# A gated recurrent attention and feed-forward kernel: fixed order on every engine, q turned by TensorE, stack halves by GpSimd, convolution sums in PSUM

## Chip, core and metric

The kernel runs on one core of a Trainium2 chip. The core has a matrix engine (TensorE; its weight loads have a row of their own), VectorE, ScalarE and GpSimd, and DMA engines that are fed from the queue of SyncE (SP) and, for a few transfers, from ScalarE's. In the rows they are PE and PEld, DVE, ACT, POOL and SPq. TensorE writes to PSUM, eight banks of 2 KB per partition; the others work on SBUF, and VectorE and ScalarE on PSUM as well. The metric is the device time of one execution in microseconds.

## What is computed

Two layers, in f32. The first is a recurrence with matrix state per head (4 batches, 8 heads, 768 steps, 40 elements per head), the second a gated feed-forward layer over the 320 joined elements.

```python
for t in range(S):                                  # 768
    m_new = maximum(f_gate[t] + m, i_gate[t])
    f_stab = exp(f_gate[t] + m - m_new); i_stab = exp(i_gate[t] - m_new); m = m_new
    C = f_stab * C + i_stab * outer(v[t], k[t])     # 40 x 40 for each head
    n = f_stab * n + i_stab * k[t]
    y[t] = sigmoid(o_gate[t]) * (C @ q[t]) / maximum(abs(n . q[t]), 1)
gate = sigmoid(causal_conv(x, conv_w))              # x is y as 4 x 768 x 320; 5 taps along t, per channel
out  = (gate * (x @ w_val)) @ w_out
```

## The kernel before

The 768 steps are cut into six chunks `j` of 128, and each chunk into two halves `p` of 64. A chunk has four units `u`, one for each batch `b`; a unit has two groups `g`, one for each half. So there are 24 units and 48 groups, and a group treats the 8 heads of a batch for 64 steps.

**Preparation of a chunk.** `load_qk`, `load_v` and `load_o` read q, k, v and the output gate. `prep_max` (ScalarE) and `prep_scale` (VectorE) find a power-of-two scale for each row. Each f32 value is then held as a pair of f16 values, side by side in a stack tile `stk` of 3 x 40 columns for each head: `prep_hi` (GpSimd, L327) writes the high part, `prep_lo` (VectorE) writes the residual (L332) and a second copy of the high part (L341). `prep_tr` (L352) turns the stack from rows to columns by a DMA transpose on SP's queue: q goes to `tq`, k to `tk`. There are 24 stacks of q and 24 of k, two `stk` buffers, three `tk` and two `tq`. `load_k` moves a copy of k with its halves swapped into `kp`, by DMA except for the first two.

**A group.** `args` (TensorE, `psd`) and `expo` (ScalarE, `dm`) make the decay weights, `scores` (8 matmuls, `pss`) the products of q and k, `probs` (VectorE, `pt`) joins both, and `keyw` (GpSimd, `kw`) weights the keys. `heads` runs 8 matmuls into `ph`, the output, and between them 8 into `pc`, the new state, which `state_out` (ScalarE) writes beside the values in `vc`; the next group of that batch reads it from there. After two groups `norm` (VectorE), `norm_o` (GpSimd) and `gate_o` (VectorE) finish the unit, `x_tr` turns it on TensorE, and `x_copy` (ScalarE) and `x_rest` (GpSimd) put it and the last four steps of the chunk before it into `xc` and `x3`.

**Feed of a chunk.** The convolution has 5 taps for each of three channel blocks. The first tap writes the sum tile `sg` (`conv0`, GpSimd, L501; for the third block VectorE, L513), the other four add to it in SBUF (`conv`, VectorE, L514). Then follow `sigmoid` (ScalarE), `val` (TensorE, `pf`), `z_mul` (VectorE), and for each batch `outp` (TensorE, `po`), `outp_st` (ScalarE) and `out_dma`. For the last chunk the feed is made in two halves of two batches.

**Order and buffers.** A table LAGS gives each step a time relative to its group or chunk. The calls are sorted by that time and handed to a scheduler, which sets the order on each engine except SP's; `heads` keeps its own order on TensorE. PSUM is split into pools: five banks in turn for `psd`, `pss`, `px`, `pf` and `po`, two for `ph`, one for `pc`.

Of the kernel before, what the change touches and what calls it, by code (L numbers as in the profile page):

```python
# [16 lines left out]

LAGS = {  # L20
    "cons1": -5.183, "cons1d": 0, "cons2": 0.457, "cons2d": 2.675, "wgt": 3.44, "wgtd": 0.804, "close": 2.831,
    "og": -7.359, "kp": -5.611, "kpd": 1.009, "vc": -3.927, "vcd": 0.989, "nat": -14.361, "natd": 0.826,
    "sig_o": -3.584, "max": -9.51, "hi": -8.451, "lo": -6.85, "lod": 0.308, "tr": -5.254, "den": -0.323,
    "dend": 0.177, "rs": 1.457, "gate": 3.86, "x_tr": 4.721, "x_copy": 6.057, "x_rest": 7.056, "args": -3.401,
    "expo": -3.399, "scores": -2.076, "probs": -1.445, "keyw": -2.703, "state": -0.531, "state_out": 0.189,
    "heads": -0.632, "conv0": 4.698, "conv0d": 0.9, "conv": 5.393, "convd": 0.299, "sig": 8.436, "val": 8.878,
    "vald": 0.463, "z": 9.375, "zh": 9.181, "zl": 9.511, "outp": 13.042, "outpd": 0.257, "ob": 15.39, "od": 14.45,
    "sig0": -0.329, "maxd": 0.014, "early": 0.441, "conv3": 8.55, "scaled": 0, "e_conv0": 5.797, "e_conv0d": 0.226,
    "e_conv": 4.49, "e_convd": 0, "e_conv3": 3.873, "e_sig": 7.715, "e_val": 6.616, "e_vald": 0.359, "e_z": 8.556,
    "e_zh": 8.123, "e_zl": 8.811, "e_outp": 11.131, "e_outpd": 0.989, "e_ob": 9.909, "e_od": 11.211, "half": 2.582,  # L30
    "si1": 1.548, "og1": 4.264, "sig1": 4.352, "vc1": -3.33, "kpe": 0, "natq": -13.409, "natqd": 0, "qmax": -10.547,
    "qmaxd": 0.075, "qhi": -9.634, "qlo": -8.762, "qtr": -8.036, "qd": 1.073, "qmul": -9.356, "qout": -3.776,
    "kpi": 6.531, "qe1": 0.864, "nat2": 0.089, "og2": -0.141, "sig2": -0.871, "qe2": 0.725, "og3": -0.415,
    "tr3": 0.74, "kp0": -1.411, "si1q": 1, "on_act_hi": 0, "on_act_dup": 0, "on_dve_state": 0, "on_dve_out": 0,
    "on_dve_x": 0, "on_dve_xl": 0, "on_dve_rs": 0, "on_dve_kw": 0, "on_dve_zl": 0, "z@2": 13.103, "zh@2": 13.406,
# [882 lines left out]
```

## Time and profile before

| | |
|---|---|
| Median of three runs | 290.42 us (290.09 to 290.68) |
| Profiled execution, its own time | 291.05 us |
| Its span, first to last instruction | 289.30 us |
| Mean granted TensorE clock | 0.850 |
| Busy: TensorE / VectorE / ScalarE / GpSimd | 214.8 / 212.2 / 137.6 / 122.3 us |
| Share of 16 DMA engines, SP's queue | 78.4% |

Busy time is the time in which an engine works on at least one instruction. A share of the span says little by itself here, since the stages of the kernel have different limits; the rows further down therefore split the span. The granted clock is in parts of full speed, 2.4 GHz; the other level is 1.2 GHz. Times within the span are counted from its start.

### The profile page before, as it was taken

What the parts mean: (1) busy time and instruction counts of PE and PEld (TensorE: products, weight loads), DVE (VectorE), ACT (ScalarE), POOL (GpSimd) and SP (SyncE); (2) the same over time, 40 slices, a digit from 0 to 9 for tenths busy, and PEclk for the clock granted to TensorE, in tenths of its full rate; (3) what the DMA queues carried; (4) which work ended last, traced back from release to release, by engine and by line L of the source; (5) the groups of instructions that cost most, each with busy time, mean ns of one, the idle gap of its engine ahead of it and who ended that gap; (6) DMA issues with size and microseconds to landing.
All of it is one profiled execution on the core that took longest, in us unless ns stands there. A gap on an engine that the chain in (4) does not pass through costs nothing.

```text
...
## 1 busy us (share of the span) xinstructions
PE 214.8 (74%) x2301; PEld 147.8 (51%) x2301; DVE 212.2 (73%) x537; ACT 137.6 (48%) x302; POOL 122.3 (42%) x211
## 2 busy tenths in 40 slices
...
GB/s 139 151 143 202 100 181 166 193 185 134 173 176 213 212 164 145 106 179 205 168 58 113 212 212 199 109 37 136 238 150 168 104 3 2 47 44 3 91 15 76
DMA packets 145895, 38.70 MB, mean 134 GB/s; under 512 B 135176, under 2 KB 143752, under 8 KB 145864
## 3 DMA queue, kind: packets, MB, share of 16 engines
q1 hardware_dynamic: 143044, 37.76, 78.4%
...
## 4 chain that ended last, share of the span: by engine, by line
PE 38%; DVE 14%; DMA 6%; issue 6%; ACT 5%; POOL 2%; SPq 1%; DVEq 0%; ACTq 0%; POOLq 0%
PE po L567 9%; PE ph L442 6%; PE pf L546 5%; DVE sg L514 4%; PE po L568 4%; PE pf L542 3%; PE pss L389 3%; PE pf L548 2%; DMA sg<-in_o_gate_dram 2%; DVE stk L332 2%; DVE pt L396 2%; DMA tk<-stk 2%; ACT sg L528 2%; PE pf L555 2%; PE px L476 2%
## 5 line engine op out<-in xcount | busy, mean ns | idle before, releaser
L442 PE MATMUL ph<-vc,pt 128*64 128x41 f32 (+1 forms) x768 | 68.5, 257 | 18.4 <-ACT vc L424 12.3
L442 PEld LDWEIGHTS ph<-vc,pt 128*64 128x64 f32 (+1 forms) x768 | 60.8, 165 | 32.6 <-ACT vc L424 15.5
L444 PE MATMUL pc<-vc,kw 128*40 128x41 f32 (+1 forms) x704 | 51.4, 235 | 5.3 <-POOL kw L408 3.5
L389 PE MATMUL pss<-tq,tk 120*128 120x64 f16 x384 | 34.4, 266 | 23.5 <-DMA tq<-stk 6.7
L327 POOL TENSOR_SCALAR stk<-nat,scl 128x320 f16<-128x320 f32 x48 | 32.6, 685 | 43.6 <-DMA tk<-stk 23.7
L444 PEld LDWEIGHTS pc<-vc,kw 128*40 128x40 f32 (+1 forms) x704 | 45.5, 135 | 10.6 <-POOL kw L408 5.5
L408 POOL TENSOR_TENSOR kw<-kp,dm 128x320 f32<-128x320 f32 (+1 forms) x44 | 35.6, 811 | 30.5 <-PE ph L442 16.6
L389 PEld LDWEIGHTS <-tk 120*128 120x128 f16 x384 | 27.6, 132 | 31.7 <-issue 15.4
L332 DVE SCALAR_TENSOR_TENSOR stk<-nat,scl,stk 128x320 f16<-128x320 f32 x48 | 33.5, 697 | 12.6 <-POOL stk L327 12.5
L514 DVE SCALAR_TENSOR_TENSOR sg<-xc,cwt,sg 128x512 f32<-128x512 f32 (+1 forms) x56 | 39.9, 730 | 3.2 <-POOL sg L501 3.1
L396 DVE SCALAR_TENSOR_TENSOR pt<-pss,cmp,dm 128x512 f32<-128x512 f32 x48 | 35.4, 738 | 9.4 <-PE ph L442 6.8
L362 PE MATMUL psd<-ra,la 120*128 120x512 bf16 x48 | 22.9, 477 | 21.5 <-DMA la<-gda 18.5
L373 ACT ACTIVATE dm<-psd 128x512 f32<-128x512 f32 x48 | 28.5, 595 | 20.5 <-PE psd L362 8.8
L293 ACT ACTIVATE junk<-nat 128x320 bf16<-128x320 f32 x48 | 22.5, 468 | 30.4 <-DMA nat<-in_q_dram 17.0
L424 ACT COPY vc<-pc 40x328 f32<-40x328 f32 x44 | 18.6, 423 | 32.9 <-PE ph L442 18.3
L462 POOL TENSOR_TENSOR rs<-sg,den 128x320 f32<-128x320 f32 x24 | 19.1, 795 | 33.6 <-DVE den L457 23.7
L567 PE MATMUL po<-wo,zt 128*128 128x320 f32 x96 | 31.3, 456 | 0.0
L573 ACT COPY ob<-po 128x320 f32<-128x320 f32 x24 | 10.0, 424 | 38.5 <-PE po L568 24.6
L560 DVE TENSOR_TENSOR zt<-pf,sg 128x512 f32<-128x512 f32 (+2 forms) x21 | 11.3, 544 | 14.8 <-PE pf L548 10.5
L546 PE MATMUL pf<-xc,wv 128*128 128x512 f32 x40 | 20.2, 629 | 2.3 <-ACT x L486 2.3
L567 PEld LDWEIGHTS po<-wo,zt 128*128 128x128 f32 x96 | 17.3, 196 | 8.8 <-issue 3.8
L501 POOL TENSOR_SCALAR sg<-xc,cwt 128x512 f32<-128x512 f32 (+1 forms) x14 | 10.7, 768 | 17.6 <-DVE zt L560 14.8
...
## 6 DMA issues: line engine op xcount, KB each, us to landing
nat<-in_q_dram SPq DMA_DIRECT2D x24, 160.0 KB, 4.1
...
out_dram<-ob SPq DMA_DIRECT2D x24, 160.0 KB, 1.8
kp<-nat SPq DMA_DIRECT2D x22, 160.0 KB, 3.0
...
nat<-in_k_dram SPq DMA_DIRECT2D x4, 160.0 KB, 3.4
rawv<-in_moe_w_val_dram SPq DMA_DIRECT2D x4, 160.0 KB, 3.3
```

Of the source, the lines that this page charges most:

```text
L327: return nc.gpsimd.tensor_scalar(o, v, f, 1.0, op0=ALU.mult, op1=ALU.mult)
L332: nc.vector.scalar_tensor_tensor(t[:, :, lo : lo + D], part(j, x, i), scl[j % 2][:, x, i : i + 1], t[:, :, 0:D], op0=ALU.mult, op1=ALU.sub ...
L362: nc.tensor.matmul(psd, la[:, p, j, b], ra[:, :, j], start=True, stop=True,)
L373: nc.scalar.activation(dm, psd_[g], AF.Exp)
L389: nc.tensor.matmul(o, tk[h], tq[:, h], start=True, stop=True)
L396: nc.vector.scalar_tensor_tensor(pt, pss_[g], cmp_[j % 2][:, p, b : b + 1], dmt[g], op0=ALU.mult, op1=ALU.mult)
L408: (nc.vector if turn("on_dve_kw", b) else nc.gpsimd).tensor_mul(kw[0:n], kp[0:n, p, b * H : (b + 1) * H], dmt[g][0:n, :, L - 1 : L].to_bro ...
L442: nc.tensor.matmul(pht[u][p * L : (p + 1) * L, h], ptt[g][0:n, h], mv, start=True, stop=True)
L444: nc.tensor.matmul(pc[n0 : n0 + D, h], kwt[g][0:n, h], mv, start=True, stop=True)
L514: nc.vector.scalar_tensor_tensor(o, x, w, o, op0=ALU.mult, op1=ALU.add)
L546: nc.tensor.matmul(pf, wv[:, c, ms], x[:, c, :, 4:], start=(c == 0), stop=False)
L567: nc.tensor.matmul(pf, zz[0][:, c, b], wo[:, c], start=(c == 0), stop=False)
```

## The change

All pools, the scheduler and LAGS go. Each step is entered in a list under a kind and a running number, and a table PLAN gives every entry a place; the list is sorted by place, and every engine executes its own instructions in that order. A second table BANKS names one of the eight PSUM banks for every sum, so any bank can serve any step.

The 24 stacks of q and the four of k's first chunk are turned by TensorE, eight transposes into one f16 bank (`turn_pe`), and copied out by ScalarE (`turn_out`); the other 20 stacks of k still go by DMA. `prep_hi` writes both copies of the high part at once, so `prep_lo` keeps one instruction. All 24 moves into `kp` are GpSimd copies. The convolution's first tap goes from GpSimd (third block: VectorE) to ScalarE and writes a PSUM bank; taps 2 to 4 add there, and the last writes `sg`. The four last steps of a chunk are carried over for all batches at once (`halo`, 10 copies for 40). The third output weight block gets its own zero-padded tile `wo3`. There are more buffers: `tk` 4 for 3, `stk` 3 for 2, `dm` 4 for 3, `pt`, `kw` and `ob` 3 for 2.

```diff
+NTK, NSTK, NDM, NPT, NKW, NOB, OJ = 4, 3, 4, 3, 3, 3, 3
+PLAN = {
+    "ld_g": "6 0",
+    "sct": "166 358 598 699 917 989",
...
+BANKS = {
+    "turn": "1023543544261302344310373663",
...
+def TURN(j, x, i):
+    return 1 if x == 0 or j == 0 else 0
+def KP(j, p, i):
+    return 2
...
-    ctx.enter_context(tc.manual_schedule(engines={mybir.EngineType.SP}))
+    ctx.enter_context(tc.manual_schedule())
...
-        put = nc.scalar.copy if j == i == 0 else nc.vector.tensor_copy if j < T["kpe"] else nc.sync.dma_start
+        put = (nc.sync.dma_start, nc.scalar.copy, nc.gpsimd.tensor_copy, nc.vector.tensor_copy)[KP(j, p, i)]
...
-    def prep_hi(j, i, x):
-        o, v, f = stk[i % 2][:, x, :, 0:D], part(j, x, i), scl[j % 2][:, x, i : i + 1]
-        return nc.gpsimd.tensor_scalar(o, v, f, 1.0, op0=ALU.mult, op1=ALU.mult)
+    def prep_hi(j, x, i):
+        t, f = stack(j, x, i), scl[j % 2][:, x, i : i + 1]
+        o = t[:, :, 0:K3].rearrange("p h (c d) -> p h c d", d=D)[:, :, 0 : 2 + x : 1 + x]
+        v = part(j, x, i)[:, :, None, :].to_broadcast([P, H, 2, D])
+            nc.gpsimd.tensor_scalar(o, v, f, 1.0, op0=ALU.mult, op1=ALU.mult)
...
-        put = nc.scalar.copy if j > 0 and turn("on_act_dup", 2 * i + x) else nc.vector.tensor_copy
-        return put(t[:, :, dup : dup + D], t[:, :, 0:D])
...
+    def turn_pe(n, j, x, i):
+        t = bank("turn", n, 512).bitcast(F16).rearrange("p (h n) -> p h n", h=H)
+        pw[j, x, i] = t
+        for h in range(H):
+            nc.tensor.transpose(t[0:K3, h], stack(j, x, i)[:, h, 0:K3], ident16)
+
+    def turn_out(j, x, i):
+        put = nc.scalar.copy if TURN(j, x, i) == 1 else nc.vector.tensor_copy
+        put(turned(j, x, i)[0:K3], pw[j, x, i][0:K3])
...
+    def conv(n, j, c, t, b0, b1):
...
+        if t == 0:
+            nc.scalar.activation(o, x, AF.Copy, scale=w)
+        else:
+            nc.vector.scalar_tensor_tensor(
+                of(gt, c, b0, b1) if t == 4 else o, x, w, o, op0=ALU.mult, op1=ALU.add
+            )
...
+    order = range(len(work)) if not slot else sorted(range(len(work)), key=lambda n: slot[work[n][0]][work[n][1]])
+    for n in order:
+        kind, i, fn, a = work[n]
+        fn(*a)
```

Three places of the order follow, each as it stands before and after. In their rows a line number, the operation, the tile written, the tiles read and the shape are named; `pb` is a PSUM bank.

SP's queue in the opening, before: after the loads of the first q and k come two transposes, then the gathers of the gate terms `ra` and `la`.

```order
L193 DMA nat_81<-in_k_dram 128x8x40
L352 DMA_TRANSPOSE tq_231<-stk_112 128x8x128
L352 DMA_TRANSPOSE tk_98<-stk_112 128x8x128
L206 DMA vc_84<-in_v_dram 64x32x40
L275 DMA ra<-gdg_122 24x8x64
L277 DMA la<-gda_124 24x4x64 x2
L206 DMA vc_84<-in_v_dram 64x32x40
L352 DMA_TRANSPOSE tq_231<-stk_113 128x8x128
```

The same place after:

```order
L367 DMA sg<-in_o_gate_dram 128x32x40
L351 DMA nat_67<-in_q_dram 128x8x40
L351 DMA nat_67<-in_k_dram 128x8x40
L355 DMA nat_68<-in_q_dram 32x8x160 x2
L343 DMA la<-gda_138 24x4x64
L339 DMA ra<-gdg_136 24x8x64
L343 DMA la<-gda_138 24x4x64
L355 DMA nat_68<-in_q_dram 32x8x160 x2
```

The transposes are gone from this queue, the output gate and part of the next q stand ahead of the gathers, and the first transpose of the program comes much later, for k of the second chunk.

TensorE at the first scores of chunk 2, before: the second group's scores (`pss_1351`) follow the first group's (`pss_1285`) with only an `args` between, and q has come by DMA.

```order
L389 LDWEIGHTS tk_100
L389 MATMUL pss_1285<-tq_951,tk_100 128x4x16
L362 LDWEIGHTS la
L362 MATMUL psd_1337<-ra,la 128x512
L389 LDWEIGHTS tk_100
L389 MATMUL pss_1351<-tq_951,tk_100 128x4x16
```

TensorE ahead of the scores of chunk 2, after: the value product of chunk 0 (L616, L607, L609) stands here, and then the first transposes of chunk 2's q (L447).

```order
L616 MATMUL pb_127<-xc_78,wall 64x256 x4
L616 MATMUL pb_127<-x_80,wall 64x256 x2
L607 MATMUL pb_125<-xc_78,wall 128x512 x2
L609 MATMUL pb_125<-x_80,wall 128x256 x2
L607 MATMUL pb_130<-xc_78,wall 128x512 x2
L609 MATMUL pb_130<-x_80,wall 128x256 x2
L447 LDWEIGHTS stk_92
L447 MATMUL pb_124<-ident_66,stk_92 120x128
```

Before, the first value product comes behind the first scores and heads of chunk 2. After, 16 of the 28 turned stacks come behind the 16th group of heads. At the other end, 32 value matmuls and 18 of the first two products of `outp` come behind the last heads before, 18 and 10 after.

VectorE at the first stack of the opening, before: the residual (L332) is followed by the second copy of the high part (L341), as every residual is.

```order
L305 TENSOR_SCALAR cmp_101<-amx_110 64x1 x2
L710 COPY la<-tl 120x2x512
L711 COPY ra<-tr 120x8x64
L332 SCALAR_TENSOR_TENSOR stk_112<-nat_81,scl_108,stk_112 128x8x40
L341 COPY stk_112<-stk_112 128x8x40
```

VectorE in the preparation of chunk 2, after: a residual (L424) stands alone, behind the last taps of chunk 0 (L575; a tap adds into a bank, a block's last one writes `sg`) and steps that convert the weights (L649 to L656).

```order
L575 SCALAR_TENSOR_TENSOR sg<-x_80,cwt,pb_126 128x256
L575 SCALAR_TENSOR_TENSOR pb_129<-xc_78,cwt,pb_129 128x512
L654 SCALAR_TENSOR_TENSOR wall<-cv_146,cv_145 128x320
L575 SCALAR_TENSOR_TENSOR sg<-xc_78,cwt,pb_129 128x512
L649 TENSOR_SCALAR cv_145<-raw_143 128x320
L650 SCALAR_TENSOR_TENSOR cv_145<-raw_143,cv_145 128x320
L656 SCALAR_TENSOR_TENSOR wall<-cv_147,wall 128x320
L651 TENSOR_SCALAR cv_146<-cv_145 128x320
L424 SCALAR_TENSOR_TENSOR stk_91<-nat_67,scl_97,stk_91 128x8x40
```

The second copy has left VectorE for GpSimd's wider `prep_hi`. Of the taps 2 to 5, 4 stand ahead of the 16th group of heads now.

## Rows read from the trace of the kernel before

**Rows 1.** Three stretches: length; PE, PEld, DVE, ACT, POOL busy; clock; DMA share; GB/s.

```profile
0.00:18.50 18.50, 0.00 (x0) 0.00 (x0) 15.97 (x54) 7.20 (x17) 12.34 (x33) 1.00 0.79 136
18.50:115.00 96.50, 54.58 (x716) 43.32 (x717) 76.72 (x201) 49.09 (x112) 45.44 (x73) 0.66 1.09 174
115.00:289.30 174.30, 160.18 (x1588) 104.48 (x1586) 119.55 (x284) 81.33 (x173) 64.55 (x106) 0.94 0.65 111
```

**Rows 2.** The same view of shorter stretches, with the same columns.

```profile
18.50:46.00 27.50, 13.68 (x185) 10.61 (x185) 24.10 (x60) 15.88 (x33) 10.38 (x19) 0.74 1.03 167
...
80.00:115.00 35.00, 20.82 (x262) 16.62 (x261) 31.57 (x77) 17.01 (x41) 20.82 (x30) 0.60 1.15 185
115.00:150.00 35.00, 28.69 (x349) 20.50 (x349) 29.35 (x76) 21.39 (x49) 18.36 (x28) 0.77 0.98 148
150.00:183.00 33.00, 30.66 (x368) 20.74 (x365) 22.30 (x53) 19.33 (x44) 14.42 (x24) 0.95 0.98 167
183.00:207.00 24.00, 23.80 (x272) 15.50 (x271) 19.21 (x52) 10.81 (x20) 13.06 (x24) 1.00 0.77 118
```

**Rows 3.** Waits of the whole span: us in total, times, longest.

```profile
POOL stk L327 <- DMA tk<-stk: 23.7, 10, 4.9
...
POOL stk L327 <- DMA tq<-stk: 8.7, 5, 2.8
```

**Rows 4.** DMA issues: count, KB each, median us to landing.

```profile
kp<-nat SPq DMA_DIRECT2D x22, 160.0 KB, 3.0
...
tq<-stk SPq DMA_TRANSPOSE x24, 3.8
tk<-stk SPq DMA_TRANSPOSE x24, 4.8
```

**Rows 5.** Timeline of the opening: start, us, engine, line, what.

```profile
13.66 1.95 SPq L275 DMA_DIRECT2D ra<-gdg  x1
...
15.80 0.77 SPq L277 DMA_DIRECT2D la<-gda  x2
...
18.54 0.59 PE L362 MATMUL psd<-ra,la 120*128 120x512 bf16 x1 [18.54 <-DMA la<-gda]
```

**Rows 6.** Chain that ended last (start, us); L476's ns min/median/max.

```profile
231.57 0.55 PE pss L389 x8
...
255.24 0.48 PE px L476 x3
...
L476 PE MATMUL px<-ident,x x72: 272/273/475, 52.8 to 258.4; 128*128 128x128 f32 x48, 128*64 128x128 f32 x24
```

**Rows 7.** Groups by form: busy us, mean ns | idle before, releaser.

```profile
L514 DVE SCALAR_TENSOR_TENSOR sg<-xc,cwt,sg 128x512 f32<-128x512 f32 x40 | 32.8, 823 | 2.5 <-POOL sg L501 2.5
...
L327 POOL TENSOR_SCALAR stk<-nat,scl 128x320 f16<-128x320 f32 x48 | 32.6, 685 | 43.6 <-DMA tk<-stk 23.7 <-DMA tq<-stk 8.7 <-DVE scl L300 5.3
...
L332 DVE SCALAR_TENSOR_TENSOR stk<-nat,scl,stk 128x320 f16<-128x320 f32 x48 | 33.5, 697 | 12.6 <-POOL stk L327 12.5
...
L341 DVE COPY stk<-stk 128x320 f16<-128x320 f16 x48 | 14.8, 307 | 0.0
...
L202 ACT COPY kp<-nat 64x640 f32<-64x640 f32 x2 | 1.4, 722 | 0.0
```

**Rows 8.** VectorE in the middle stretch: L341's instructions alone, then L514's.

```profile
18.50:115.00 96.50, 5.32 (x23) 0.66 1.09 174
...
18.50:115.00 96.50, 8.43 (x12) 0.66 1.09 174
```

**Rows 9.** Lines L396, L332, L514: ns min/median/max, first and last start.

```profile
L396 DVE SCALAR_TENSOR_TENSOR pt<-pss,cmp,dm x48: 693/738/753, 22.1 to 245.1; 128x512 f32<-128x512 f32 x48
...
L332 DVE SCALAR_TENSOR_TENSOR stk<-nat,scl,stk x48: 493/550/1133, 9.1 to 221.3; 128x320 f16<-128x320 f32 x48
...
L514 DVE SCALAR_TENSOR_TENSOR sg<-xc,cwt,sg x56: 466/737/1633, 88.9 to 269.7; 128x512 f32<-128x512 f32 x40, 128x256 f32<-128x256 f32 x16
```

**Rows 10.** Chain that ended last: start, us, the last heads.

```profile
252.18 1.06 PE ph L442 x16
```

More of the change, by code (lines that the diff above doesn't have):

```diff
@@ new lines, in tile_mlstm_gated_ffn, with op, bank @@
+    x_ = ring(2, [P, H, D], F32, "x")
+    obt = cst.tile([P, NOB * DM], F32, name="ob")
+    ob_ = [obt[:, i * DM : (i + 1) * DM] for i in range(NOB)]
+    pb = [ps.tile([P, 512], F32, name=f"pb{i}") for i in range(8)]
+    work, seen = [], {}
+    def op(kind, fn, *a):
+        i = seen[kind] = seen.get(kind, -1) + 1
+        work.append((kind, i, fn, a))
+    turns = {}
+    def bank(kind, i, n, m=None):
+        if kind in BANKS:
+            b = int(BANKS[kind][i])
+        else:
+            b = turns["b"] = (turns.get("b", -1) + 1) % 8
+        t = pb[b][:, 0 : n * (m or 1)]
+        return t.rearrange("p (a b) -> p a b", b=m) if m else t
@@ L569, in outp @@
-        pot[(j, b)] = pf
+        r = slice(0, P) if j < NJ - 1 else half(b)
+        nc.tensor.matmul(pf, zz[1][r, b % B2], wo3[r, b // B2], start=False, stop=True)
     def outp_st(j, b):
-        ob = wk.tile([P, DM], F32, name=f"ob{j}_{b}", tag="ob", bufs=2)
-        (nc.vector.tensor_copy if turn("on_dve_out", b) else nc.scalar.copy)(ob, pot[(j, b)])
-        pot[(j, b)] = ob
+        nc.scalar.copy(ob_[(j * B + b) % NOB], pot[j, b])
     def out_dma(j, b):
-        nc.sync.dma_start(out[b, j * P : (j + 1) * P, :], pot[(j, b)])
@@ L882, in tile_mlstm_gated_ffn @@
-    for j in range(NJ - 1):
-        feed(j, (j + 1) * SJ, 0, B)
-    for i in range(2):
-        feed(NJ - 1, NG + T["half"] * i, 2 * i, 2 * i + 2, "e_")
-    for _, _, fn, a in sorted(work, key=lambda w: w[:2]):
+            if x == 0:
+                nc.vector.tensor_reduce(sel_b, i4, axis=AX.X, op=ALU.add)
+            else:
+                nc.vector.tensor_reduce(sel_g, i4.rearrange("p b g -> p g b"), axis=AX.X, op=ALU.add)
+    MS, VS = nc.gpsimd.memset, nc.vector.memset
+    op("ld_g", nc.sync.dma_start, fg, f_gate.rearrange("b h s -> (b h) s"))
@@ new lines, in tile_mlstm_gated_ffn @@
+    op("c_p", make_identity, nc, ident)
+    op("c_v", nc.vector.tensor_copy, ident16, ident)
+    op("c_p", MS, io_, 0.0)
+    for r0 in (0, 2 * D):
+        op("c_p", fill, io_[:, 0:D], [[-1, D]], -r0)
+    for i in range(NTK):
+        for x in range(2):
+            op("idk", idk, i, x)
+    for x in range(2):
+        op("sums", sums, x)
+    op("c_p", MS, kp[0:L, 0], 0.0)
+    for p in range(2):
+        op("kp_c", kp_const, p)
+    for i in range(2):
+        op("c_p", MS, vc[i][0:L, 0], 0.0)
+        for p in range(2):
+            op("c_p", MS, vc[i][TOK[p] : TOK[p] + L, p, :, D:DT], 1.0)
@@ new lines, in feed_part @@
+    def feed_part(j, b0, b1):
+        for c in range(3):
+            n = seen.get("conv0", -1) + 1
+            for t in range(5):
+                op("conv" if t else "conv0", conv, n, j, c, t, b0, b1)
+        op("sig", sigmoid, j, b0, b1)
+        for m in range(3):
+            op("val", val, seen.get("val", -1) + 1, j, m, b0, b1)
+            op("z", z_mul, j, m, b0, b1)
+        for b in range(b0, b1):
+            op("outp", outp, j, b)
+            op("ob", outp_st, j, b)
+            op("od", out_dma, j, b)
```

974 lines of the change are left out of this document (459 added, 515 removed), and 74 rows, old and new, of tables (LAGS, PLAN).

## The prediction

> **What bounds the kernel now.** I read the trace by stretches first, because no engine is the limit throughout. [rows 1] cuts the span where the first TensorE work starts (18.5 us) and where 16 of the 48 head groups are done (115 us; counted from the `ph` matmuls). The reader is to compare each engine's busy time with the length of its stretch. In the middle stretch (96.5 us) TensorE is busy 54.6, at a granted clock of 0.66, ScalarE 49.1 and GpSimd 45.4; VectorE is busy 76.7, and the DMA engines stand at 1.09 of their capacity. In the last stretch (174.3 us) TensorE is busy 160.2: it is the bound there, with the DMA share down to 0.65. [rows 2] refines that: VectorE reaches 0.88 (24.10 of 27.50) and 0.90 (31.57 of 35.00) of two slices of the middle, and at 115 to 150 us it is still level with TensorE (29.35 and 28.69 of 35); from 150 us TensorE is at 0.93 and then 0.99, with the clock back at 1.00.
>
> Next I asked what keeps VectorE from being full in the middle. The waits [rows 3] name DMA transposes: GpSimd stands 23.7 and 8.7 us because the stack buffers it must refill are still being read by a transpose. A transpose lands 3.8 or 4.8 us after its issue [rows 4], and two stack buffers do not cover that. So the middle is bound by VectorE through a chain that DMA latency keeps opening, and the end by TensorE.
>
> **The change part by part.** The sum is made against the profiled execution: span 289.30 us, its own time 291.05, so 1.75 lies around the span. Its time is 0.63 above the median of the three runs, 290.42.
>
> *Opening, 18.5 us.* The gathers of the gate terms are issued at 13.66 and 15.80 us, behind two transposes on SP's queue, and TensorE's first matmul waits for the last of them until 18.54 [rows 5]. The new queue has no transpose ahead of them. The latest gather can go out about 2.1 us earlier (15.80 to 13.66), but VectorE and GpSimd get more constants and wider stacks first. Bounds 16.4 and 18.5; I take 17.5.
>
> *Transposes of q and of the first k.* 28 of 48 leave the DMA queue. On TensorE each is 8 matmul-type instructions of 128 columns, f16. No row shows that form. From below: the eight score matmuls, with the same kind of weight load but 64 columns, take 0.55 us [rows 6]. From above: three f32 transposes of 128 columns take 0.48, so eight take 1.28 [rows 6]. I take 0.75, nearer the row of the same type. 12 of the 28 lie before group 16, where TensorE has 42 us to spare in the middle stretch alone; 16 lie in the last stretch, where they are on the path: 16 x 0.75 = 12 us, bounds 8.8 and 20.5. The single row of an f32 transpose reads 0.273 us [rows 6] although three take 0.48, so the length of one is not its price in a row of eight. The Trainium skill, VectorE: DVE Perf Modes, "The three transpose paths", gives 390 ns for one 128x128 transpose on TensorE; taken as a rate, an estimate, that would be 50 us for those 16 stacks and a slower kernel, but the pair of rows just named speaks for a length.
>
> Each of the 28 needs a copy out of PSUM on ScalarE, 120x1024. ScalarE's copy of 64x640 takes 0.722 us [rows 7], so in proportion at most 1.16 us, 32 us in all. The 21 first taps that ScalarE takes over are at most 512 wide, each below that 0.722: at most 15 more. ScalarE is busy 7.2 + 49.1 + 81.3 = 137.6 us now [rows 1], at most 185 after: 0.67 of the new span. I cost it at nothing; TensorE's and VectorE's fuller time covers it, and where an `expo` or a state copy queues behind such a copy with TensorE dry, it costs up to 1.16 each time.
>
> *Stack halves.* VectorE's 48 duplicate copies go, 0.307 us each [rows 7]: 5.32 us of the middle stretch [rows 8]. GpSimd writes both instead, 640 elements for 320: 0.685 us now [rows 7], after it between 0.8 and 1.37. That is 5 to 33 us more. The 24 `kp` copies add some 19, at the 0.8 of a 640-element operation (ScalarE takes 0.722 for this copy). GpSimd goes from 12.3 + 45.4 + 64.6 = 122.3 us [rows 1] to at most 175, before its first taps and most halo copies leave: 0.64 of the new span at most. `keyw` no longer waits for a `kp` DMA (22 of these, 3.0 us to land, [rows 4]) but sits behind GpSimd's own copies, in order. I price the queueing at nothing, and the effect on VectorE's residuals as a rival.
>
> *Convolution sums in PSUM.* A tap now reads one tensor from SBUF, not two. `probs` already has that shape (PSUM in, one SBUF tensor): 693 to 753 ns at 128x512, never more; a convolution tap on two SBUF tensors runs from 466 to 1633, and the residual of a stack from 493 to 1133 [rows 9]. The Trainium skill, SBUF — State Buffer, "SBUF: two separate sides", says that VectorE instructions with two SBUF inputs and GpSimd instructions shut each other out of a shared pair of ports. By that rule, the trace agrees, the taps settle at 738 ns; and it speaks against the change too, as the residuals keep two SBUF inputs and GpSimd reads more (a rival below).
>
> The 40 wide taps have a mean of 823 [rows 7], so 85 ns each is gained, 3.4 us in all and only 0.3 in the middle, because of 12 taps done there now (8.43 us) [rows 8] only 4 stand before group 16 in the new order; the other 8, 5.6 us, move to where TensorE is the bound.
>
> *Middle stretch.* VectorE's work: 76.7 - 5.3 - 5.6 - 0.3 = 65.5 us. With 12 fewer transposes to wait for, a third stack buffer and a fourth `tk`, I take the use that it already reaches in two slices, 0.89: 74 us instead of 96.5. TensorE needs 54.6 + 12 x 0.75 = 63.6 of it even at the low clock, so it fits, barely. Bounds: at today's use (0.795) 82 us; at TensorE's limit 67.
>
> *Last stretch.* TensorE: 160.2 + 12 = 172. At 115 to 150 us the clock granted is 0.77, at 150 to 183 us 0.95 [rows 2]: 28.69 x 0.23 + 30.66 x 0.05 = 8 us would come back at full clock throughout; I take half. Idle is 14.1 now. The slice at 115 holds 6.3 of that, with VectorE as full as TensorE; relief there and eight shared banks give back perhaps 4. The tail takes it again: now 36 us of stored feed work follow the last head group at 252.18 us [rows 10] and hide its chain; the new order leaves 18 value matmuls and 10 of the first two output products behind it instead of 32 and 18, while the chain (normalize, gate, transpose, 12 taps of at least 0.466 us [rows 9], so 5.6, then sigmoid, product, two outputs) is not shorter. I cost that at 4, between 0 and twice that, since the taps are the only part without TensorE work to fill it. So 172 - 4 + 14 = 182. Bounds: 160.2 + 8.8 - 8 + 10 = 171, and 174.3 + 20.5 + 4 = 199.
>
> **Sum:** 17.5 + 74 + 182 = 273.5; with 1.75 around the span 275.25; at the median about 275 us. The gain is made before group 16 (23.5 us) and partly given back after it (8).
>
> **The rivals.**
>
> *TensorE keeps its full clock and the order is tight:* 16.4 + 71 (65.5 at 0.92) + 171 = 258.4, so about 259. For it: [rows 2] shows full clock where TensorE was 0.99 busy, and the middle gets denser. Against: TensorE still waits on VectorE there.
>
> *GpSimd stretches VectorE's residuals:* each residual behind a wider GpSimd operation. If 23 in the middle take the longest of 1.133 instead of 0.697 [rows 7, 9], that is 10 us more: 75.5 at 0.89 = 85. Then 17.5 + 85 + 182 = 284.5, about 286. For it: [rows 9]; this is the page's port rule at work. Against: the taps, which share the effect today, leave it.
>
> *Slower: the last stretch pays more than the middle gains.* The transposes of later chunks at 1.28 each, the copy-out late on ScalarE's queue, so that TensorE dries, and a middle that stays at 0.795: 18.5 + 82 + 199 = 299.5, about 300. With the middle at 74 it decides from a last stretch of 198 us, a growth of 23.5; with the middle at 82 already from 190, where 16 transposes at 1.0 with no clock returned stand (174.3 + 16). For it: [rows 1], TensorE has 14 us to spare there in all. Against: feed work can fill, as chunk 0's value product comes before any score of chunk 2.
>
> **How the numbers follow.** Forecast 0.60, at 275, its own range 264 to 285. Full clock 0.16, at 259. Residuals stretched 0.10, at 286. Slower 0.12, at 300. Nothing measurable 0.02. The range 257 to 290 leaves out the slower case and the outer side of the fast one, 0.17 together. A measurement of this kernel tells 0.2%, about 0.6 us, from no change: faster by more 0.85, within 0.02, slower 0.13.
>
> **What would show it.** Group 16 done at about 91 us, with VectorE near 0.89 in the middle; GpSimd's waits for transposes near zero; eight f16 transposes in 0.55 to 1.28 us; taps at 128x512 all between 0.69 and 0.76; TensorE 172 us busy or a little less after group 16. It is wrong if group 16 is done later than 100 us, if the last stretch exceeds 190 us, or if the residual's mean rises above 0.9 us.

## The result, and the profile after

| | before | after |
|---|---|---|
| Median of four runs, same chip | 290.25 us (289.58 to 290.68) | 262.23 us (259.25 to 263.82) |
| Ratio, 95% interval | | 0.896 (0.890 to 0.902) |
| Profiled execution: own time, span | 291.05, 289.30 us | 263.5, 261.6 us |
| Mean granted TensorE clock | 0.850 | 0.935 |
| Busy: TensorE / VectorE / ScalarE / GpSimd | 214.8 / 212.2 / 137.6 / 122.3 us | 209.9 / 201.6 / 170.9 / 134.0 us |
| Share of 16 DMA engines, SP's queue | 78.4% | 63.7% |

The changed kernel is 10% faster: about 28 us, where the forecast of 275 us had 15. Its four times fall in pairs, 259.25 and 260.96, 263.5 and 263.82, and the ratio compares the faster pair; the expectations below therefore take 260 us for it, while the profile shown is of an execution some 3 us above. The experiments have their own runs of the kernel before beside them, so their ratios are what to compare.

The stretches that answer to [rows 1] are cut at the first matmul of the gate terms (27.8 us) and just behind the last heads of the 16th group, which end at 90.8 us (columns as there):

```profile
0.00:27.80 27.80, 5.88 (x48) 5.33 (x49) 19.43 (x56) 13.64 (x24) 19.95 (x41) 1.00 0.95 142
27.80:91.70 63.90, 45.58 (x730) 37.55 (x728) 56.14 (x129) 50.78 (x116) 43.32 (x56) 0.76 0.95 144
91.70:261.60 169.90, 158.45 (x1752) 113.21 (x1750) 126.01 (x278) 106.44 (x213) 70.70 (x96) 0.99 0.49 86
```

The opening, which answers to [rows 5] (timeline; in brackets idle time and what ended it):

```profile
12.27 6.65 ACTq L332 DMA_DIRECT2D gda<-gsp  x4
...
19.58 0.47 ACT L376 ACTIVATE junk<-nat 128x320 bf16<-128x320 f32 x1 [10.29 <-DMA gda<-gsp]
...
22.85 0.53 SPq L343 DMA_DIRECT2D la<-gda  x1
...
26.12 1.96 PE L447 MATMUL pb<-ident,stk 128*120 128x128 f16 x16 [0.67 <-DVE stk L424]
27.87 1.06 PE L459 MATMUL pb<-ra,la 120*128 120x512 bf16 x2
```

The first matmul of the gate terms comes 9.3 us later than before. ScalarE stands for 10.3 us behind the DMAs that it issues itself, and the row maximum of the second batch's k waits behind them, with the next stacks, their transposes and TensorE in turn.

The groups that answer to [rows 7] (busy us, mean ns | idle before, releaser), and behind them the row of the waits that answers to [rows 3] (us in total, times, longest):

```profile
L575 DVE SCALAR_TENSOR_TENSOR pb<-xc,cwt,pb 128x512 f32<-128x512 f32 x30 | 22.1, 744 | 0.1
...
L424 DVE SCALAR_TENSOR_TENSOR stk<-nat,scl,stk 128x320 f16<-128x320 f32 x48 | 32.4, 692 | 1.8 <-POOL stk L420 1.7
...
L420 POOL TENSOR_SCALAR stk<-nat,scl 128x640 f16<-128x640 f32 x48 | 45.7, 962 | 26.6 <-PE pb L447 9.3 <-DVE scl L382 6.6 <-DMA tk<-stk 5.1
...
L447 PE MATMUL pb<-ident,stk 128*120 128x128 f16 x224 | 21.2, 256 | 27.3 <-DVE stk L424 26.7 <-DVE zt L621 0.7
...
L451 ACT COPY tq<-pb 120x1024 f16<-120x1024 f16 x24 | 23.9, 1009 | 8.4 <-PE pb L447 8.2
```

```profile
POOL stk L420 <- DMA tk<-stk: 5.1, 4, 2.3
```

TensorE's transposes (L447) alone, up to the 16th group and behind it (length; busy of PE and PEld; clock, DMA share, GB/s):

```profile
0.00:91.70 91.70, 11.41 (x96) 9.98 (x96) 0.83 0.95 143
91.70:261.60 169.90, 9.74 (x128) 8.74 (x128) 0.99 0.49 86
```

Taps now last 744 ns, residuals 692 as before (697), and GpSimd waits 5.1 us for DMA transposes where it waited 32.4.

**Where the 28 us are.** The 16th group turned out a poor mark (below), so the span is cut at the first instruction of the 24th and of the last `probs`: up to the middle of the groups, from there to the last group, and the tail of feed work behind it. Before, then after:

```profile
0.00:139.50 139.50, 75.32 (x980) 57.73 (x980) 113.15 (x302) 72.93 (x164) 70.66 (x124) 0.74 1.03 167
139.50:245.10 105.60, 98.56 (x1149) 67.19 (x1150) 75.90 (x184) 52.53 (x112) 47.28 (x81) 0.94 0.78 127
245.10:289.30 44.20, 40.88 (x180) 22.88 (x176) 23.19 (x54) 12.16 (x27) 4.39 (x6) 0.98 0.12 45
```

```profile
0.00:127.80 127.80, 82.98 (x1172) 66.32 (x1173) 108.04 (x254) 91.37 (x186) 88.44 (x127) 0.87 0.93 144
127.80:233.70 105.90, 102.66 (x1251) 76.01 (x1246) 77.88 (x170) 69.32 (x142) 44.08 (x63) 1.00 0.45 79
233.70:261.60 27.90, 24.28 (x110) 13.78 (x110) 15.67 (x40) 10.17 (x23) 1.45 (x2) 1.00 0.10 36
```

The tail is 16.3 us shorter: 16.6 us of TensorE's work (40.88 to 24.28) has gone from it to places between the groups. How the rest divides depends on the mark. By these rows the middle did not grow for that, although it holds 4.1 us more of TensorE's work, and the first row lost 11.7 us, in spite of the late start. Cut where the heads of the same two groups end (150.5 and 253.2 us before, 130.4 and 237.9 after), the first part loses 20.1 us, the middle grows by 4.8 and the tail loses 12.4. What needs no mark is TensorE's total: it is busy 4.9 us less, although 21.2 us of transposes came to it, and idle 22.8 us less (74.5 to 51.7 us). The experiments ask what makes room for the moved work: the order, or the parts of the change that came with it.

### The profile page after: what moved, and what is told of

It is laid out like the page before. It is cut to its first block, busy times and chain, and to the rows that moved or that the text cites. A ratio compares the mean times of both kernels' runs of the same rounds, so it can differ in the third digit from the quotient of the medians.

```text
span 261.6 us, 6597 instructions
## 1 busy us (share of the span) xinstructions
PE 209.9 (80%) x2525; PEld 156.1 (60%) x2525; DVE 201.6 (77%) x461; ACT 170.9 (65%) x349; POOL 134.0 (51%) x191
## 3 DMA queue, kind: packets, MB, share of 16 engines
q1 hardware_dynamic: 112904, 27.06, 63.7%
## 4 chain that ended last, share of the span: by engine, by line
PE 54%; DVE 16%; DMA 11%; ACT 7%; SPq 5%; issue 4%; POOL 2%; ACTq 0%; DVEq 0%; POOLq 0%
PE pb L506 11%; PE pb L626 9%; PE pb L477 7%; DMA sg<-in_o_gate_dram 7%; PE pb L628 5%; PE pb L607 4%; DMA nat<-in_q_dram 4%; PE pb L604 4%; PE pb L459 3%; PE pb L447 3%; DVE pt L482 2%; SPq L351 2%; PE pb L536 2%; PE pb L609 2%; DVE stk L424 2%
## 5 line engine op out<-in xcount | busy, mean ns | idle before, releaser
L506 PE MATMUL pb<-vc,pt 128*64 128x41 f32 (+1 forms) x768 | 57.0, 240 | 8.3 <-DVE pt L482 7.1
L506 PEld LDWEIGHTS pb<-vc,pt 128*64 128x64 f32 (+1 forms) x768 | 51.6, 147 | 18.5 <-issue 6.9
L420 POOL TENSOR_SCALAR stk<-nat,scl 128x640 f16<-128x640 f32 x48 | 45.7, 962 | 26.6 <-PE pb L447 9.3
L508 PE MATMUL pb<-vc,kw 128*40 128x41 f32 (+1 forms) x704 | 45.7, 221 | 2.1 <-ACT vc L515 1.1
L482 DVE SCALAR_TENSOR_TENSOR pt<-pb,cmp,dm 128x512 f32<-128x512 f32 x48 | 34.7, 747 | 15.1 <-PE pb L477 7.8
L447 PE MATMUL pb<-ident,stk 128*120 128x128 f16 x224 | 21.2, 256 | 27.3 <-DVE stk L424 26.7
L508 PEld LDWEIGHTS pb<-vc,kw 128*40 128x40 f32 (+1 forms) x704 | 40.7, 122 | 2.4 <-POOL kw L489 1.2
L447 PEld LDWEIGHTS <-stk 128*120 128x120 f16 x224 | 18.7, 163 | 31.0 <-DVE stk L424 28.1
L626 PE MATMUL pb<-wall,zt 128*128 128x320 f32 x96 | 32.2, 457 | 2.4 <-DVE zt L621 2.4
L424 DVE SCALAR_TENSOR_TENSOR stk<-nat,scl,stk 128x320 f16<-128x320 f32 x48 | 32.4, 692 | 1.8 <-POOL stk L420 1.7
L376 ACT ACTIVATE junk<-nat 128x320 bf16<-128x320 f32 x48 | 22.5, 470 | 15.0 <-DMA gda<-gsp 10.3
L477 PE MATMUL pb<-tq,tk 120*128 120x64 f16 x384 | 29.1, 251 | 2.7 <-DMA tk<-stk 1.5
L462 ACT ACTIVATE dm<-pb 128x512 f32<-128x512 f32 x48 | 27.6, 595 | 3.4 <-PE pb L459 2.2
L526 POOL TENSOR_TENSOR rs<-sg,den 128x320 f32<-128x320 f32 x24 | 18.9, 789 | 18.5 <-DVE den L522 18.0
L575 DVE SCALAR_TENSOR_TENSOR pb<-xc,cwt,pb 128x512 f32<-128x512 f32 (+1 forms) x42 | 27.9, 669 | 0.3
L621 DVE TENSOR_TENSOR zt<-pb,sg 128x512 f32<-128x512 f32 (+2 forms) x21 | 11.1, 547 | 17.5 <-PE pb L609 9.3
L626 PEld LDWEIGHTS pb<-wall,zt 128*128 128x128 f32 x96 | 17.5, 196 | 10.2 <-DVE zt L621 2.5
```

The lines of the kernel that those rows point to most:

```text
L420: nc.gpsimd.tensor_scalar(o, v, f, 1.0, op0=ALU.mult, op1=ALU.mult)
L424: nc.vector.scalar_tensor_tensor(t[:, :, lo : lo + D], part(j, x, i), scl[j % 2][:, x, i : i + 1], t[:, :, 0:D], op0=ALU.mult, op1=ALU.sub ...
L447: nc.tensor.transpose(t[0:K3, h], stack(j, x, i)[:, h, 0:K3], ident16)
L462: nc.scalar.activation(dm_[g % NDM], psd[g], AF.Exp)
L477: nc.tensor.matmul(o, tk[h], tq[:, h], start=True, stop=True)
L482: nc.vector.scalar_tensor_tensor(pt_[g % NPT], pss[g], cmp_[j % 2][:, p, b : b + 1], dm_[g % NDM], op0=ALU.mult, op1=ALU.mult)
```

## The experiments

Theory A: the removed work and waits (transposes by DMA, copies on VectorE, slow taps) are the gain, and the order only places it. Rival B: order and shared banks are the gain, since they keep TensorE fed. For the opening, theory C: it is on the path; rival D: VectorE takes it back.

### e1: q by DMA again

The 20 stacks of q of chunks 1 to 5 are turned by DMA, at the places in the order that TensorE's transposes had.

```diff
 def TURN(j, x, i):
-    return 1 if x == 0 or j == 0 else 0
+    return 1 if j == 0 else 3 if x == 0 else 0
...
+        if TURN(j, x, i) == 3:
+            return prep_tr(j, x, i)
```

> The changed kernel with the 20 stacks of q of chunks 1 to 5 turned by DMA transposes again, at the places that the TensorE transposes had in the order; the rest as changed. Its fast runs take about 260 us. Theory A (the DMA transposes' latency was what held the middle): GpSimd waits for transposes again, 5.1 us now to 20 or more, group 16 is done later than 105 us (100 now), 270 to 280 us. Rival B (the order and the shared banks made the gain; q by DMA would be hidden, and TensorE loses 20 x 0.57 = 11.4 us of work): 250 to 262 us, TensorE busy about 199 for 210.

Measured: 277.48 us, ratio 0.955 (0.950 to 0.960): 17 us lost. The three rows as above, then waits between 88 and 128 us:

```profile
0.00:136.30 136.30, 76.80 (x1096) 59.56 (x1096) 110.20 (x254) 82.25 (x181) 86.51 (x126) 0.85 0.95 152
136.30:246.70 110.40, 101.37 (x1159) 73.73 (x1159) 76.48 (x170) 59.75 (x128) 45.33 (x65) 0.95 0.56 102
246.70:275.20 28.50, 24.28 (x110) 13.77 (x110) 15.63 (x40) 10.16 (x23) 1.44 (x2) 0.98 0.10 35
```

```profile
POOL stk L420 <- DMA tq<-stk: 7.4, 3, 3.6
DVE stk L424 <- POOL stk L420: 6.7, 3, 3.1
...
PE pb L481 <- DMA tq<-stk: 4.2, 1, 4.2
```

Theory A's size, but not its place. GpSimd's waits for transposes are back at 20.2 us in all (16.5 for `tq`, 3.7 for `tk`). TensorE has 7.5 us less to do (202.4 us busy in all) and the run is longer all the same. The 16th `probs` start at 90.4 us for 88.2 after, only 2 us later, and the heads of that group end at 92.7 us for 90.8 (the 100 us that the expectations of this run and of e3 give for the changed kernel is a misreading); the 17th, the first of chunk 2, start at 121.5 for 113.4. The transposes that hurt are those of chunk 2's q, and the waits are the ones named in [rows 3], moved there.

### e2: the order alone

The edits of e1, e5 and e6 together, and 22 of the 24 copies into `kp` by DMA. The first chunk's transposes on TensorE, the joint `halo` copies, `wo3` and the further buffers stay as changed, so a little more than the order is left:

```diff
 def KP(j, p, i):
-    return 2
+    return 1 if j == i == 0 else 0
```

> The changed kernel's order, banks and buffers alone: q of chunks 1 to 5 by DMA, the second copy of the high part on VectorE, the convolution summed in SBUF with its first taps on GpSimd, 22 of 24 copies into kp by DMA, all as before the change. Theory A (removed work and waits made the gain): 283 us or more, since 14.8 us of copies and 3.4 us of slower taps are on VectorE again and the transposes are waited for. Rival B (order and banks made at least half of it): 275 us or less.

Measured: 286.55 us, ratio 0.987 (0.981 to 0.992), as theory A expects. Its three rows:

```profile
0.00:141.10 141.10, 80.02 (x1070) 61.90 (x1071) 114.35 (x287) 79.64 (x172) 70.16 (x114) 0.82 1.01 165
141.10:256.00 114.90, 103.06 (x1192) 74.91 (x1189) 84.67 (x189) 56.73 (x123) 46.57 (x61) 0.96 0.58 107
256.00:283.80 27.80, 24.28 (x110) 13.69 (x110) 17.64 (x42) 7.49 (x17) 3.83 (x6) 0.99 0.10 36
```

The order alone brings the short tail (27.8 us), and pays for it: 9.3 us in the middle row and 1.6 in the first, by these marks.

### e7: parts in the old order

Three parts of the change put into the kernel before; the convolution and the first chunk's transposes stay as they were. The main edit:

```diff
+        if x == 0 and j > 0:
+            pt = ps_s.tile([P, H, P], F16, name=f"tp{j}_{i}", tag="big")
+            for h in range(H):
+                nc.tensor.transpose(pt[0 : 3 * D, h], stk[i % 2][:, x, h, 0 : 3 * D], ident16)
+            nc.scalar.copy(t[0 : 3 * D], pt[0 : 3 * D])
+            return
         nc.sync.dma_start_transpose(t, stk[i % 2][:, x].rearrange("p h n -> p (h n)"))
```

> The kernel before with three parts of the change and its own scheduler and PSUM pools: the 20 stacks of q of chunks 1 to 5 turned by TensorE and copied out by ScalarE, both copies of the high part written by GpSimd, and the copies into kp by GpSimd from chunk 1 on. Theory A (the removed work and waits are the gain, the order only places it): 268 to 276 us for 290. Rival B (they pay only with the fixed order and banks that any step can use: here the copies out of PSUM queue on ScalarE, and a transposed stack takes one of five banks in turn): 283 us or more.

Measured: 291.5 us, ratio 1.007 (1.003 to 1.011): no gain at all. Its three rows, and its residuals:

```profile
0.00:140.70 140.70, 78.84 (x1130) 62.51 (x1131) 122.09 (x280) 87.37 (x188) 91.06 (x140) 0.92 0.97 140
140.70:244.30 103.60, 97.51 (x1162) 66.52 (x1160) 73.98 (x159) 56.91 (x107) 56.57 (x86) 0.97 0.48 81
244.30:288.40 44.10, 40.85 (x178) 22.80 (x174) 23.17 (x54) 12.17 (x27) 4.40 (x6) 1.00 0.13 45
...
L335 DVE SCALAR_TENSOR_TENSOR stk<-nat,scl,stk 128x320 f16<-128x320 f32 x48 | 35.2, 744 | 5.8 <-POOL stk L330 5.7
```

Rival B's size. The tail stays at 44.1 us, the first row is no shorter, and VectorE's busy time in it is 122.1 us for 113.2, although its copies had left: its instructions got longer (the residuals' mean is 744 ns for 697), while GpSimd did more (152.0 us busy for 122.3). TensorE's clock rose from 0.74 to 0.92 in the first row without one microsecond of gain. So e2 gains 1.3%, e7 nothing, and both together, with the convolution, 10.4%: it is neither theory, but the pair. The order moves the work, and the parts make the room. One rival is left: each order was made for its own parts. The list gives a DMA transpose the place of one on TensorE, and the LAGS are those of the old parts. A list made for the old parts, or LAGS made for the new ones, was not run, so how much of the pair's gain is such a misfit stays open.

### e5, e6 and e10: VectorE's two parts, one at a time

e5, in `prep_hi` and `prep_lo`:

```diff
-        o = t[:, :, 0:K3].rearrange("p h (c d) -> p h c d", d=D)[:, :, 0 : 2 + x : 1 + x]
-        v = part(j, x, i)[:, :, None, :].to_broadcast([P, H, 2, D])
+        o, v = t[:, :, 0:D], part(j, x, i)
...
+        nc.vector.tensor_copy(t[:, :, dup : dup + D], t[:, :, 0:D])
```

> The changed kernel with the second copy of the high part made by VectorE again, 48 copies of about 0.307 us, and GpSimd's high part 320 wide again. Theory A (VectorE binds up to the 16th head group): the 23 or so copies before it, 5 to 7 us, are on the path, 265 to 268 us for 260, and little comes from the copies after it, where TensorE binds. Rival B (GpSimd is what the stacks wait for, and it gets 13 us back): 258 to 261 us.

Measured: 262.43 us, ratio 0.904 (0.897 to 0.911), not to be told from 0.896 (0.890 to 0.902). The 16th `probs` start at 88.2 us, as in the changed kernel. Up to there, after the change and then in e5:

```profile
0.00:88.20 88.20, 47.96 (x709) 40.09 (x711) 72.91 (x175) 62.26 (x131) 62.16 (x94) 0.83 0.95 143
```

```profile
0.00:88.20 88.20, 46.75 (x710) 39.08 (x711) 75.94 (x190) 61.08 (x128) 54.08 (x93) 0.85 0.96 141
```

Rival B's time holds: VectorE (the third busy time) does 3.0 us more in the same stretch, so the exchange is worth nothing measurable: the copy was not on the path, or GpSimd's shorter part pays for it.

e6, in `conv`:

```diff
-        o = pg[j, c, b0]
+        o = of(gt, c, b0, b1)
...
-            nc.scalar.activation(o, x, AF.Copy, scale=w)
...
+            (nc.gpsimd if c < 2 else nc.vector).tensor_scalar(o, x, w, 1.0, op0=ALU.mult, op1=ALU.mult)
...
```

> The changed kernel with the convolution summed in SBUF as before the change: first taps on GpSimd (third block: VectorE), the other taps on two SBUF tensors, at the same places of the order. Theory A (taps lie where TensorE binds, and only their mean falls, 85 ns each for 40): 260 to 263 us for 260. Rival B (two SBUF inputs and GpSimd's first taps stretch each other and sit ahead of the last product): some taps above 0.9 us again, the last chunk's feed later, 264 to 270 us.

Measured: 273.07 us, ratio 0.943 (0.936 to 0.950): 13 us lost, more than either side expected. e10 asks which half of that edit did it: first taps on ScalarE, sums in SBUF.

```diff
-        o = pg[j, c, b0]
+        o = of(gt, c, b0, b1)
...
+            nc.vector.scalar_tensor_tensor(o, x, w, o, op0=ALU.mult, op1=ALU.add)
```

> The changed kernel with the convolution summed in SBUF, but the first taps on ScalarE as changed. e6, which also gave the first taps to GpSimd and VectorE, took 273.1 us for about 260, with a mean of 957 ns for a 128x512 tap (744 with sums in PSUM). Theory A (a tap with two SBUF inputs is stretched while GpSimd works, and GpSimd works more since the change): the mean stays at 900 ns or more with a longest above 1500, 267 to 272 us. Rival B (the first taps on GpSimd and VectorE made e6 slow): mean below 850 ns, 260 to 264 us.

Measured: 271.26 us, ratio 0.936 (0.930 to 0.943). The taps by form, of e6 and of e10:

```profile
L575 DVE SCALAR_TENSOR_TENSOR sg<-xc,cwt,sg 128x512 f32<-128x512 f32 x40 | 37.9, 957 | 1.8 <-POOL sg L573 1.5
```

```profile
L575 DVE SCALAR_TENSOR_TENSOR sg<-xc,cwt,sg 128x512 f32<-128x512 f32 x40 | 35.8, 904 | 1.0 <-ACT sg L573 0.8
```

Theory A: it is the taps with two SBUF inputs. Under the new order one costs 904 to 957 ns on average, the longest 1917, for 744 with the sum in PSUM; in the kernel before it was 823 [rows 7]. The mean goes with GpSimd's work: under the new order it is 862 ns in e2 (GpSimd busy 120.5 us), 904 in e10 (142.6) and 957 in e6 (152.8). No run changes GpSimd's work alone, so that it is the cause is argued. The loss lies mostly between the 24th and the last group, where e6 takes 111.5 us and e10 110.9 for 105.9.

### e3, e4, e9: the opening

e3 moves entries of the table only: the loads of q and k ahead, and the row maxima ahead of ScalarE's DMA issues.

```diff
-    "ld_q0": "14 10 20 52 62 56 95 100",
+    "ld_q0": "14 10 20 21 22 22 23 23",
...
-        "39 44 48 79 90 93 121 155 160 ...
+        "39 44 48 49 50 51 52 53 160 ...
```

> The changed kernel with two moves in the opening: the loads of all q and k of chunk 0 stand ahead of those of v and the output gate on SP's queue, and ScalarE's eight row maxima of chunk 0 stand ahead of the five issues that write the gate terms to DRAM, behind which ScalarE stands 10.3 us now (from 9.3 to 19.6). Theory C (the opening is on the path; it got longer with the change): the first probs start at 23 to 27 us instead of 31.6, and the whole run is 4 to 8 us shorter, 252 to 256. Rival D (VectorE, at 33.4 of 34 us between 46 and 80, takes it back): group 16 is done at 99 to 101 as now, within 1.5 us of 260.

Measured: 254.85 us (254.49 to 255.84), ratio 0.877 (0.874 to 0.880). That beats both kernels. Its first matmul of the gate terms with the transposes ahead of it (timeline), and its three rows:

```profile
21.31 1.96 PE L447 MATMUL pb<-ident,stk 128*120 128x128 f16 x16 [0.67 <-DVE stk L424]
23.06 1.06 PE L459 MATMUL pb<-ra,la 120*128 120x512 bf16 x2
```

```profile
0.00:121.80 121.80, 81.31 (x1175) 65.08 (x1177) 108.89 (x255) 91.60 (x186) 88.20 (x127) 0.87 0.99 152
121.80:224.90 103.10, 101.75 (x1248) 75.54 (x1243) 77.76 (x170) 69.18 (x142) 44.04 (x63) 1.00 0.42 80
224.90:252.80 27.90, 24.28 (x110) 13.78 (x110) 15.63 (x40) 10.16 (x23) 1.44 (x2) 0.97 0.10 36
```

Theory C: the first `probs` start at 26.9 us for 31.6, the 16th at 81.1 for 88.2, and nothing takes it back. Loads and row maxima were moved together, so their shares stay open.

e4 also puts the output gate's load and the next q behind the gathers:

```diff
-    "ld_o": "64 338 ...
+    "ld_o": "120 338 ...
...
-    "sig_o": "97 386 224",
+    "sig_o": "158 386 224",
```

> As the run before it, and the output gate's first load and the loads of the next q stand behind the gathers of the gate terms, with the sigmoid of the output gate behind the second exponential. Theory C2 (the 640 KB of the output gate and the next q delay the gathers): the first matmul of the gate terms starts 2 to 4 us earlier than in that run (27.8 now), the time is 2 to 3 us less still. Rival D2: the gathers wait for the writes on ScalarE's queue alone, and the late sigmoid holds up GpSimd's product of the first unit: no gain over that run, or 1 to 2 us lost.

Measured: 256.02 us, ratio 0.883 (0.878 to 0.889), no better than e3. The last gather goes out at 18.0 us instead of 21.5, but the matmul of the gate terms still starts at 23.15: in TensorE's order it stands behind the third pair of stacks' transposes, which start at 21.39, and these do not need the gathers. Rival D2 has the time, but neither side of the expectation named this reason.

e9, on the kernel of e3, puts the writes of the gate terms on SP's queue instead, and the first loads of v and the output gate behind them:

```diff
-        nc.scalar.dma_start(
+        (nc.scalar if i else nc.sync).dma_start(
             gda[i].rearrange("h x p j b t -> b h (x p j) t")[b],
```

> The kernel of e3 (254.9 us) with the five issues that write the gate terms of the first chunk to DRAM on SP's queue instead of ScalarE's, directly behind the loads of q and k, and the loads of v and the output gate behind them. In e3 the last gather goes out at 21.5 us and the first matmul of the gate terms starts at 23.1. Theory C (the gate terms' way through DRAM is what the first groups wait for): that matmul starts at 17 to 20 us, the first probs 2 to 4 us before e3's 26.9, and the time is 251 to 253. Rival D (v, 640 KB and now later, or ScalarE's own row of copies and table loads ends last): first probs within 1 us of 26.9, time within 1 us of 254.9.

Measured: 261.87 us, ratio 0.905 (0.900 to 0.910); first `probs` at 32.4 us. Worse than both sides expected. Its timeline:

```profile
18.43 4.85 SPq L355 DMA_DIRECT2D nat<-in_q_dram  x2
...
23.39 0.35 SPq L343 DMA_DIRECT2D la<-gda  x1
...
25.57 1.27 ACT L591 ACTIVATE sg<-sg 128x1280 f32<-128x1280 f32 x1 [6.77 <-DMA sg<-in_o_gate_dram]
```

The gathers stand behind two loads whose issue alone held SP for 4.85 us, and ScalarE waits 6.8 us for the output gate, with four copies out of PSUM behind it. Here the gate terms do bind: TensorE waits 4.3 us for the gather of `ra`, until 27.5 us.

### e8: more work for TensorE's clock

On the kernel of e3:

```diff
-        nc.tensor.matmul(psd[g], la[:, p, j, b], ra[:, :, j], start=True, stop=True)
+        for _ in range(3 if 4 <= g < 16 else 1):
+            nc.tensor.matmul(psd[g], la[:, p, j, b], ra[:, :, j], start=True, stop=True)
```

> The kernel of e3 (254.9 us) with the matmul of the gate terms made three times instead of once in head groups 4 to 15: 24 more of 512 columns, 0.4 to 0.55 us each, 10 to 13 us of TensorE work that changes no value. In e3 TensorE's granted clock is 0.52 between 44 and 64 us, with TensorE busy 13.3 of 20 us. Theory E (the low clock follows TensorE's pauses and stretches what VectorE waits for): the clock between 44 and 64 us rises above 0.75, and the time does not grow, 252 to 255. Rival F (VectorE, busy 19.65 of those 20 us, binds whatever the clock): the clock may rise, the time stays within 1 us of 254.9. Rival G: the added matmuls lie on the path, 257 us or more.

Measured: 256.87 us, ratio 0.887 (0.882 to 0.893), 2 us more than e3. The stretch of e3, then of e8:

```profile
44.00:64.00 20.00, 13.34 (x147) 11.61 (x146) 19.65 (x51) 13.26 (x32) 10.09 (x13) 0.52 0.92 149
```

```profile
44.00:64.00 20.00, 12.51 (x125) 9.72 (x126) 19.69 (x49) 12.93 (x30) 10.25 (x12) 0.53 0.85 140
```

The clock stays at 0.53, but theory E was not put to the test: only four of the 24 added matmuls start in this stretch, and TensorE's busy time in it did not grow. The time lies between rivals F and G. So the run shows what such padding costs here, and not whether a busier stretch would keep its low clock.

### e11 and e12: banks and stack buffers

```diff
-            b = int(BANKS[kind][i])
...
+        r = {"ph": "h", "pc": "c"}.get(kind, "s")
+        n0, nb = {"h": (5, 2), "c": (7, 1), "s": (0, 5)}[r]
+        turns[r] = turns.get(r, -1) + 1
+        b = n0 + turns[r] % nb
```

> The changed kernel with PSUM split as before the change: heads' outputs in two banks in turn, the state in one, everything else in five in turn. Order and parts as changed. Theory A (that any bank serves any step is what lets the feed's products stand between head groups): TensorE idles more between the 16th and the 48th group (7.8 us now), 268 us or more. Rival B (the order alone does that): 259 to 264 us.

```diff
-NTK, NSTK, NDM, NPT, NKW, NOB, OJ = 4, 3, 4, 3, 3, 3, 3
+NTK, NSTK, NDM, NPT, NKW, NOB, OJ = 4, 2, 4, 3, 3, 3, 3
...
```

> The changed kernel with two stack buffers instead of three. Theory A (the third buffer is what keeps VectorE at 0.88 of its time up to the 16th group): GpSimd waits for stacks longer, the 16th probs start 3 us or more later than the 88.2 of now, 264 to 270 us. Rival B (transposes by TensorE free a stack so early that two do): within 2 us of 260, and the 16th probs at 87 to 90.

Measured: 280.15 us, ratio 0.955 (0.947 to 0.962), and 267.1 us, ratio 0.921 (0.908 to 0.933). Both are inconclusive. The list is made for eight banks and three stacks; with fewer, some sums and stacks are written over before they are read, so these kernels compute something else, and a writer no longer waits for the readers that it should wait for. What the banks or the third buffer are worth by themselves stays open.

## Why the prediction was right, and where it was not

The sign and the range held; the centre was 13 us too slow. The parts of the sum erred in both directions: against the profiled span the opening was 10.3 us longer than forecast, the middle 10.1 and the last stretch 12.1 us shorter.

**Opening: 17.5 us forecast, 27.8 measured.** The step "The latest gather can go out about 2.1 us earlier" failed; the last one went out at 22.85 us instead of 15.80 [rows 5]. The order in front of the prediction shows the output gate and the next q ahead of the gathers, and that was priced at nothing; but e4, which puts them behind, gains nothing over e3. The term that the sum lacks is the chain ahead of the first gate matmul in TensorE's order: loads, row maxima behind ScalarE's DMA issues, stacks, and three pairs of transposes. e3 shortens it: five table entries for loads and five for row maxima, together, were worth 5.6 us (0.896 to 0.877 of 290).

**Middle: group 16 at 91 us forecast, its last heads done at 90.8, VectorE's use 0.88 for 0.89.** The number is right for the wrong reasons. The late opening cost 10 us. On the other side, VectorE had 75.6 us of work up to the mark (19.43 + 56.14), not the 81.5 of the sum: it had done 27 residuals up to the mark before and 16 up to the mark after, as chunk 2's preparation now stands behind the mark. The forecast had read that 16 of 28 transposes lie behind it and moved the taps, but it left the residuals of those stacks in VectorE's term. The mark itself was also misread: before the change the heads of the 16th group end at 109.3 us, and at 115 us the 17th group has begun. Measured alike, group 16 is done 18.5 us earlier, but the first `probs` of the 17th start at 113.4 us after and at 113.0 before. TensorE between the two, before and then after:

```profile
109.30:113.80 4.50, 0.44 (x3) 0.09 (x2) 4.45 (x11) 1.02 (x3) 3.63 (x6) 1.00 0.73 156
```

```profile
90.80:115.40 24.60, 20.09 (x133) 13.36 (x132) 22.39 (x53) 16.10 (x29) 15.63 (x19) 0.93 0.71 121
```

Work of 20 us of TensorE's time, the value product of chunk 0 and the transposes of chunk 2's q among it, now stands behind the mark and before the 17th group. A mark by groups done is only fair when the same work lies before it on both sides, and neither the 16th nor the 24th group is such a mark; "The gain is made before group 16" can be neither confirmed nor denied by it.

**The waits for transposes.** GpSimd's waits went nearly to zero as forecast, and e1 shows that taking away those for q is worth 17 us in this order. But they did not set the time to group 16: with q by DMA it is 2 us later. The loss comes mainly at the change to chunk 2 (2 us at the 16th `probs`, 8 at the 17th), whose q must be turned before its first scores.

**VectorE's copies and taps.** The copies were priced at 5.3 us in the middle; e5, which gives them back for GpSimd's narrower instruction, shows nothing measurable. A use of 0.88 was not saturation, as VectorE carried 3.0 us more there in the same time. The taps were priced at 85 ns each, 3.4 us, and measure 744 ns for 823, as forecast. But the comparison that counts is with a tap in SBUF under the new order, 904 to 957 ns, and e6 and e10 put the whole at 11 to 13 us. The row of before understated it; GpSimd did less there. This agrees with the rule of the Trainium skill that the forecast drew on (SBUF — State Buffer, "SBUF: two separate sides": VectorE instructions with two SBUF inputs and GpSimd's that read SBUF shut each other out): more work on GpSimd makes the escape to PSUM worth more. The rival built on it, longer residuals, did not come (692 ns for 697), though in e7 they rose to 744.

**Last stretch: 182 us forecast, 169.9 measured, 12 us too slow.** TensorE was put at 172 less 4 for the clock, 168, and is busy 158.5; idle was put at 14 and is 11.5. Of the 9.5 us of work, 4 are the clock, of which half was credited (8 us against full speed) and nearly all came (0.94 to 0.99); 2.3 are the transposes, 9.7 us of their own time for 12; both are estimates, and the rows don't split the remaining 3. The tail has the wrong sign: "The tail takes it again", at 4 us, while the time behind the last heads fell from 36.1 to 23.7 us. The smaller store of feed work behind the last heads was read as lost cover; it was work done earlier, where TensorE had stood idle: by the rows cut at `probs`, its busy time rose by 7.7 us up to the 24th group and by 4.1 from there to the last, with its idle time falling from 64.2 to 44.8 and from 7.0 to 3.2 us.

**Price of a stack's transposes:** behind the 16th group eight took 0.61 to 0.66 us, near the lower bound and below the 0.75 of the sum; up to it ten of the twelve took 1.06 to 1.11, so that the twelve cost 11.4 us for the 9 of the sum, where TensorE had time to spare. **ScalarE at nothing:** right behind the opening, 170.9 us busy, and TensorE waits 0.3 us for its copies. **Full clock, tight order, 259 us** was the nearest rival, in its time and in its clock after the 16th group (0.99), but with an opening 11 us longer than it supposed.
